# One DMA queue for v, later weight sums, a pause of attention pieces, and warming matmuls in a fused attention and expert kernel

## The chip, the cores and the metric

The kernel runs on one core of a Trainium2 chip. The metric is the device time of one execution in microseconds (us), and quoted times are medians of several executions. "Span" is the time from the first to the last instruction in one profiled execution; it is about 1.8 us shorter than the device time. A ratio is the mean time of one kernel's fast runs over the mean of the other's fast runs of the same rounds, so it isn't quite the ratio of the medians.

## The reference

Polynomial-sketch attention on q, k, v of shape (4, 4, 1088, 32), then four experts on its 4352 rows of 128:

```python
def phi(x):                                   # 8 x 8 = 64 features
    a = np.einsum('rd,bhsd->bhsr', S1, x); b = np.einsum('rd,bhsd->bhsr', S2, x)
    return np.einsum('bhsi,bhsj->bhsij', a, b).reshape(*x.shape[:-1], r * r)
q_p, k_p = phi(q), phi(k)
kv  = np.einsum('bhsf,bhsd->bhfd', k_p, v);  z = np.sum(k_p, axis=2)
x   = (q_p @ kv) / (q_p . z + 1e-6)           # bridged to (4352, 128)
p   = domain_probs / (domain_probs.sum(-1, keepdims=True) + 1e-9)
for e in range(4):
    h = np.maximum(x @ w1[e], 0.0);  out += p[:, e:e+1] * (h @ w2[e])
```

All inputs and the output are float32.

## The kernel before

The experts' work runs in eleven chunks of columns of x (128, 480, 480, five of 512, ...), each in 16 steps. `first(i)` of a step makes h and rectifies it; `second(i - 2)` multiplies by w2. The attention for later columns is a generator of "pieces", and `work()` spends a credit on them between the matmuls of `first`. GpSimd (POOL) forms sums of blocks of w2, which `second` needs from chunk 1 on. PE is TensorE, DVE VectorE, ACT ScalarE and SP SyncE. Names in the traces: kn and kT are k as loaded and transposed, vn is v as loaded, f a projection of k or q and fs its copy, qp the products that make the features of q, kvz the sums over keys, den and num the attention's denominator and numerator, xT the finished columns of x, hid the rectified h, w2s the weight sums, and end the sum of outputs of chunk 0.

The loads at the start. The second half of v goes through ScalarE's queue:

```python
    load_rows(k, 0, "kn")
    load_rows(q, 0, "qn", slice(0, P))
    vn[0] = load_v(0, (nc.sync, nc.scalar))
    ...                                  # domain_probs, ends, rest of q, then w1 and w2 of each expert
    for _ in range(11):
        wp = psum(ps_h, "h")
        nc.tensor.matmul(wp[:, :], warm[:, 0:P], warm[:, :], start=True, stop=True)
```

The key projection, whose output tile comes from PSUM (the memory that these matmuls write), and the end of the first 128 columns of x:

```python
    def keys(b):
        ...
        for gi in range(3):
            key_project(b, gi, psum(ps_f, "f"))   # 32 or 8 matmuls, then a ScalarE copy fs<-f
            yield
    ...
        key_divide(b, kv)
        for _ in attend(b, 0, n, qp):             # den and num matmuls, then DVE: dT, rc, rb, xT
            pass
```

The main loop:

```python
            rate = CHUNKS[m] / NQ * max([0] + [(needed[c] + 4 - done[0]) / (START[c] - gone) for c in range(m + 1, NC)])

            def work():
                credit[0] = min(credit[0] + rate / 2, 2)
                while credit[0] >= 1:
                    credit[0] -= 1
                    piece()

            first(i, work)
            if i > NQ // 2:                       # NQ is 16
                next(to_sum, None)                # one weight sum on GpSimd
```

## Time and profile before

| | before |
|---|---|
| median of the first 3 runs | 502.18 us (500.72 to 502.39) |
| span of the profiled run | 500.6 us |
| TensorE busy | 491.1 us, 98% |
| first matmul on x | 15.11 us |
| stretch at half clock | 15.89 to 19.30 us |
| matmuls wait for DVE's qp products | near 26 us |
| matmuls wait at the entry of chunk 1 | near 39 and 42 us |

TensorE is the bound, so the reader looks for its holes. In the timeline each line has the start, the time taken, the engine, the line of code, the operation, output and input, and in brackets how long the engine had stood and for whom. These lines of the kernel before are from the entry of chunk 1:

```profile
36.58 0.70 DVE L458 STREAM_SHUFFLE qf<-f 128x480 f32<-128x480 f32 x1
...
41.96 0.34 DVE L642 SCALAR_TENSOR_TENSOR end<-o,ends,end 128x128 f32<-128x128 f32 x1
42.22 0.39 DVE L578 SCALAR_TENSOR_TENSOR hid<-h,hid 128x240 f32<-128x240 f32 x1
42.35 0.63 PE L185 MATMUL o<-hid,w_sb 128*64 128x240 f32 x4 [0.58 <-DVE end L642]
```

DVE works on attention pieces (qf and others) from 36.58. The last eviction of chunk 0 (end) comes only at 41.96, behind them, and the matmuls that need its PSUM bank wait.

### The profile page before, as it was taken

To read this page: it belongs to the slowest core of one execution; us is meant where nothing else is said; L and a number is where in the kernel's file an instruction comes from. 1 tells how busy PE (TensorE), PEld (TensorE's weight loads), DVE (VectorE), ACT (ScalarE), POOL (GpSimd) and SP (SyncE) were. 2 spreads that over 40 slices of the span, in tenths; PEclk is the share of its full clock that TensorE was granted. 3 is DMA by queue.
4 is the path that set the end of the run, shared out by engine and by line. 5 is a ranking of instruction groups with operands and counts; after the bars stand their busy time and mean duration, and the time that the engine had idled before them with its cause. 6 is when DMAs were issued, how large, how long until landed. Compare 5 with 4: busy or idle time off the path is not lost.

```text
span 500.6 us, 11017 instructions
## 1 busy us (share of the span) xinstructions
PE 491.1 (98%) x4431; PEld 368.2 (74%) x4431; DVE 324.7 (65%) x751; ACT 243.8 (49%) x487; POOL 228.2 (46%) x259
## 2 busy tenths in 40 slices
PE   8899999999999999999999999999999999999996
PEld 5775888777776657777777777777777777788996
DVE  5659665867667575757667646558656557665642
ACT  3233454545554464544545455445455445566651
POOL 6620334444544263444545344344555355655570
PEclk9899999999999999999999999999999999999999
DMA  7981030021002230021001100021001100110000
GB/s 184 300 289 55 1 91 1 2 85 20 1 2 84 67 89 1 1 85 22 1 2 62 44 1 1 2 85 22 2 1 52 23 1 0 45 22 3 14 3 17
DMA packets 29618, 22.36 MB, mean 45 GB/s; under 512 B 19968, under 2 KB 26752, under 8 KB 29184
## 3 DMA queue, kind: packets, MB, share of 16 engines
q1 hardware_dynamic: 29264, 21.40, 14.9%
q8 instruction: 35, 0.57, 0.5%
q10 hardware_dynamic: 304, 0.26, 0.2%
q14 instruction: 15, 0.12, 0.1%
HBM read 19.35 MB, written 2.31 MB: 43 GB/s over the span
## 4 chain that ended last, share of the span: by engine, by line
PE 94%; DMA 2%; DVE 2%; SPq 0%; issue 0%; ACT 0%; ACTq 0%
PE h L185 47%; PE o L185 39%; PE f L185 4%; PE den L185 2%; DMA w_sb<-in_moe_w_dram 1%; PE num L185 1%; DMA vn<-in_v_dram 1%; DVE qp L409 1%; DVE hid L578 1%; SPq L147 0%; DVE qa L468 0%; DVE qf L458 0%; DVE qb L463 0%; DVE qf L460 0%; DVE end L642 0%
## 5 line engine op out<-in xcount | busy, mean ns | idle before, releaser
L185 PE MATMUL h<-xT,w_sb 128*64 128x512 f32 (+4 forms) x1408 | 299.6, 497 | 1.9 <-DMA w_sb<-in_moe_w_dram 1.6
L578 DVE SCALAR_TENSOR_TENSOR hid<-h,hid 128x256 f32<-128x256 f32 (+6 forms) x432 | 203.6, 472 | 149.3 <-ACT hid L603 141.0
L603 ACT ACTIVATE hid<-h 128x512 f32<-128x512 f32 (+3 forms) x288 | 158.1, 550 | 202.9 <-PE h L185 165.1
L185 PE MATMUL o<-hid,w2s 128*64 128x256 f32 (+3 forms) x1152 | 220.9, 355 | 0.0
L185 PEld LDWEIGHTS h<-xT,w_sb 128*64 128x64 f32 x1408 | 150.2, 138 | 53.0 <-issue 4.7
L185 PE MATMUL o<-hid,w_sb 128*64 128x256 f32 (+3 forms) x864 | 185.0, 356 | 0.6 <-DVE end L642 0.6
L185 PEld LDWEIGHTS o<-hid,w2s 128*64 128x64 f32 x1152 | 131.6, 137 | 31.8 <-issue 0.6
L718 POOL TENSOR_TENSOR ev<-yz,sh 64x256 f32<-64x256 f32 (+3 forms) x72 | 48.4, 673 | 157.8 <-ACT sh L721 155.1
L185 PEld LDWEIGHTS o<-hid,w_sb 128*64 128x64 f32 x864 | 101.4, 137 | 21.1 <-issue 1.6
L706 POOL TENSOR_TENSOR yz<-ev 128x512 f32<-128x512 f32 (+3 forms) x36 | 42.3, 1175 | 86.4 <-ACT ev L709 86.2
L718 POOL TENSOR_TENSOR ct<-ev 128x512 f32<-128x512 f32 (+3 forms) x36 | 42.2, 1173 | 2.8
L718 POOL TENSOR_TENSOR ct<-ct,gate 128x512 f32<-128x512 f32 (+3 forms) x27 | 31.9, 1181 | 2.1
L718 POOL TENSOR_TENSOR total<-total,ct 128x512 f32<-128x512 f32 (+3 forms) x27 | 31.7, 1175 | 2.1
L409 DVE TENSOR_TENSOR qp<-qa,qb 64x352 f32<-64x352 f32 (+2 forms) x44 | 31.3, 712 | 1.0
L185 PE MATMUL o<-w_sb,hid 128*64 128x128 f32 x256 | 24.6, 277 | 0.0
L708 ACT COPY ev<-o 128x512 f32<-128x512 f32 (+3 forms) x36 | 19.3, 537 | 9.7 <-PE o L185 9.2
L185 PEld LDWEIGHTS o<-w_sb,hid 128*64 128x64 f32 x256 | 20.7, 140 | 2.1 <-issue 1.5
L595 ACT ACTIVATE hid<-h 128x256 f32<-128x256 f32 x24 | 9.2, 383 | 24.8 <-PE h L185 24.3
L709 ACT COPY ev<-o 128x512 f32<-128x512 f32 (+3 forms) x36 | 19.4, 538 | 3.0
L348 DVE TENSOR_TENSOR kp<-fs 128x256 f32<-128x256 f32 (+1 forms) x24 | 16.1, 677 | 0.0
L721 ACT COPY sh<-yz 64x256 f32<-64x256 f32 (+3 forms) x36 | 13.7, 379 | 1.6 <-POOL yz L706 0.8
L722 ACT COPY sh<-yz 64x256 f32<-64x256 f32 (+3 forms) x36 | 13.7, 380 | 0.9
(95 smaller groups left out, 246.2 us busy)
## 6 DMA issues: line engine op xcount, KB each, us to landing
w_sb<-in_moe_w_dram SPq DMA_DIRECT2D x8, 512.0 KB, 7.5
gate<-gates SPq DMA_DIRECT2D x3, 1024.0 KB, 4.7
kn<-in_k_dram SPq DMA_DIRECT2D x4, 544.0 KB, 3.9
gate<-gates SPq DMA_DIRECT2D x2, 960.0 KB
vn<-in_v_dram SPq DMA_DIRECT2D x14, 128.0 KB, 5.8
qn<-in_q_dram SPq DMA_DIRECT2D x3, 544.0 KB, 3.6
gate<-gates SPq DMA_DIRECT2D x1, 896.0 KB
out_dram<-ob SPq DMA_DIRECT2D x12, 64.0 KB, 2.0
```

The lines of the kernel that those rows point to most:

```text
L185: nc.tensor.matmul(out(s), weights(s), moving(s), **flags)
L348: eng.tensor_tensor(out=_ap(kps[b], 0, P, 256 * t0 + P * p + 64 * x, [[256, n], [32, 2], [R, 4], [1, R]]), in0=_ap(src, 0, P, off + 4 * x, ...
L409: nc.vector.tensor_tensor(out=qp[p][64 * x : 64 * x + 64, 0:n], in0=qa[64 * p : 64 * p + 64, 0:n], in1=qb[64 * p : 64 * p + 64, 0:n], op=A ...
L578: nc.vector.scalar_tensor_tensor(out=out, in0=src, scalar=0.0, in1=in1, op0=ALU.max, op1=ALU.subtract)
L595: nc.scalar.activation(hd[:, 0 : 2 * n], hp[:, 0 : 2 * n], ACTF.Relu)
L603: nc.scalar.activation(hd[:, n * j : n * j + n], hp[:, 0:n], ACTF.Relu)
L706: add = lambda out, in0, in1, op=ALU.add: nc.gpsimd.tensor_tensor(out=out, in0=in0, in1=in1, op=op)
L708: nc.scalar.copy(_ap(ev, 0, P, 0, [[2 * w, 2], [1, w]]), _ap(a0, 0, P, 0, two))
L709: nc.scalar.copy(_ap(ev, 0, P, w, [[2 * w, 2], [1, w]]), _ap(a1, 0, P, 0, two))
L718: add = lambda out, in0, in1, op=ALU.add: nc.gpsimd.tensor_tensor(out=out, in0=in0, in1=in1, op=op)
L721: nc.scalar.copy(sh[HP:P, 0:w], yz[0:HP, 0, 0:w])
L722: nc.scalar.copy(sh[0:HP, 0:w], yz[HP:P, 1, 0:w])
```

## The change

Its intent is to take four holes out of TensorE's time: let k land alone, keep weight sums away from DVE's products, keep attention pieces away from the entry of chunk 1, and keep the clock up while x is made.

```diff
-    vn[0] = load_v(0, (nc.sync, nc.scalar))
+    vn[0] = load_v(0)                              # all of v on nc.sync
...
+    def keep_warm(n):
+        for _ in range(n):
+            wp = psum(ps_h, "h")
+            nc.tensor.matmul(wp[:, :], warm[:, 0:P], warm[:, :], start=True, stop=True)
+    keep_warm(11)
...
-        for _ in attend(b, 0, n, qp):
+        first = attend(b, 0, n, qp)
+        next(first)                                # den and num
+        keep_warm(4)
+        for _ in first:
             pass
...
-                credit[0] = min(credit[0] + rate / 2, 2)
+                if not NQ <= i < NQ + 2:
+                    credit[0] = min(credit[0] + rate / 2, 2)
...
-            if i > NQ // 2:
+            if i > NQ - 4:
                 next(to_sum, None)
```

More of the change, by code (lines that the diff above doesn't have):

```diff
@@ L93, in load_rows, with load_v @@
         nc.sync.dma_start(d[b][:, part], bass.AP(src.tensor, src.offset + b * H * S * D + c, [[G * D, P], [1, n]]))
-    def load_v(b, engines):
+    def load_v(b):
         t = lpool.tile([P, H * NT * D], F32, tag="vn", name="vn")
@@ L98, in load_v @@
         for a in range(4):
-            engines[a // 2].dma_start(
+            nc.sync.dma_start(
                 _ap(t, 32 * a, 32, 0, [[8 * D, H], [1, 8 * D]]),
@@ L113, in load_batch @@
         load_rows(k, b, "kn")
-        vn[b] = load_v(b, (nc.sync, nc.sync))
+        vn[b] = load_v(b)
         load_rows(q, b, "qn")
@@ L170 @@
         nc.gpsimd.memset(own2[32 * h : 32 * h + 32, h % 2 : h % 2 + 1], 1.0)
-    for _ in range(11):
-        wp = psum(ps_h, "h")
-        nc.tensor.matmul(wp[:, :], warm[:, 0:P], warm[:, :], start=True, stop=True)
+    def keep_warm(n):
[3 more added lines that the diff above has]
+    keep_warm(11)
     turn = [0]
```

## The prediction

> **What bounds the kernel now.** I read the page first, then the chain of waits, then the table of stretches, then the timeline of the stretches that lose time.
>
> ```profile
> PE 491.1 (98%) x4431; PEld 368.2 (74%) x4431; DVE 324.7 (65%) x751; ACT 243.8 (49%) x487; POOL 228.2 (46%) x259
> ...
> PE h L185 47%; PE o L185 39%; PE f L185 4%; PE den L185 2%; DMA w_sb<-in_moe_w_dram 1%; PE num L185 1%; DMA vn<-in_v_dram 1%; DVE qp L409 1%; DVE hid L578 1%; SPq L147 0%; DVE qa L468 0%; DVE qf L458 0%; DVE qb L463 0%; DVE qf L460 0%; DVE end L642 0%
> ```
>
> TensorE is the bound: 98% busy and 94% of the chain. Only its idle time and its slow time can be won. A busy PE is not a PE at its peak, so I also added up the columns of all 4431 matmul records at 1/2.4 us per thousand (the steady stretch from 100 to 150 us needs 49.6 us at this rate and takes 50.1). The sum is 478 us, of which the time from the first matmul to the last takes 496. The lost 18 us lie thus: 5.9 before 15 us, 1.7 between 15 and 19.3, 1.3 between 25 and 29, 1.8 between 35 and 42.5, and the rest is spread at 0.4 to 1.5 per 50 us. The change touches exactly the first four.
>
> The start, from the chain in order of time (start us, us, what):
>
> ```profile
> 1.37 4.75 DMA vn<-in_v_dram
> 6.12 0.02 issue
> 6.13 0.35 SPq L140
> 6.49 0.04 issue
> 6.53 0.70 SPq L147
> 7.23 0.04 issue
> 7.27 0.55 SPq L147
> 7.82 0.04 issue
> 7.86 0.48 SPq L93
> 8.34 0.04 issue
> 8.39 6.58 DMA w_sb<-in_moe_w_dram
> 14.97 0.14 issue
> 15.11 2.12 PE h L185 x24
> ```
>
> Two paths meet at 15.1. The load of the first w1 is issued only at 8.39, because SyncE's queue stood until 6.12 for a transfer of v issued by ScalarE, and lands at 14.97. The other path (k, its projection, key sum, division) gives x at 14.77 (the xT product starts at 14.48 and lasts 0.29). The load wins by 0.2 to 0.3 us only: both must come sooner.
>
> The table of stretches, with the granted clock as the column after POOL, and the two culprits on DVE and POOL in the timeline:
>
> ```profile
> 15.90:19.30 3.40, 3.40 (x26) 2.41 (x24) 0.80 (x4) 1.05 (x3) 2.87 (x5) 0.50 1.11 336
> 25.00:29.00 4.00, 3.82 (x35) 1.92 (x31) 3.17 (x5) 0.77 (x2) 2.84 (x3) 1.00 0.60 234
> 38.40:42.40 4.00, 3.13 (x24) 1.25 (x20) 3.93 (x12) 1.71 (x3) 0.00 (x0) 1.00 0.02 6
> ```
>
> ```profile
> 25.17 2.09 DVE L409 TENSOR_TENSOR qp<-qa,qb 64x480 f32<-64x480 f32 x2
> ```
>
> ```profile
> 25.60 1.13 POOL L491 TENSOR_TENSOR w2s<-w_sb,w2s 128x256 f32<-128x256 f32 x1
> ```
>
> PE is busy all through 15.9 to 19.3, but at half clock: 3.4 us of time, 1.7 of work. From 25 to 29 DVE's products for the second piece of x are late. From 38.4 to 42.4, the first steps of chunk 1, DVE is 98% busy (3.93 of 4.00) and PE is idle for 0.87.
>
> [...] one stretch at 0.50, 3.41 us long in the clock's record, and the window of that length before it (12.48 to 15.89) holds only 0.66 us of den and num and 0.78 of h, 42% busy. [...] a qp product takes 0.64 to 0.66 us at 41 to 47 us with POOL idle, and 1.87 and 2.09 per pair at 22.5 and 25.2 beside weight sums, which themselves go from 0.73 to 1.05-1.14. [...] this k lands near 5.7 (4.5 us after issue), the median of the four k loads is 3.9.
>
> **The change part by part.**
>
> *First v behind k in one queue.* No bytes change: k 544 KB, v 544 KB. Two ScalarE issues (0.81 us) become two SyncE issues (2 x 0.43, from its rows), which fall before the wait that ended at 6.12. [...] with the median 3.9 it lands near 5.0, 0.7 sooner. By the built order of waits, the domain_probs load, which waited for ScalarE's v, now waits for k. SyncE so resumes near 5.0 to 5.3 instead of 6.1, but the later issues wait for the first q and v pieces, and the w1 load for the third v piece, which comes later than before. I put the w1 issue at 7.5 (7.0 to 8.4), its landing at 14.1. On the x path, projection can start at 5.95 (the 11 warm matmuls end at 5.92) against 6.62; the value copies need all of v, which waited until 8.46 before and will not be sooner. Key sums, 72 matmuls in 2.30 us, can start their first half on the first copy. x at 14.1. Gain 0.6, between 0 and 1.1.
>
> *Warming while x is made.* Four bf16 matmuls of 128x512. Eleven took 4.73 us at half clock, 0.43 each; at full clock half of that, 4 x 0.215 = 0.86 us, put into the hole of 1.64 us after num (13.47 to 15.11). They end near 14.3, ahead of x, so on the path they cost nothing. The busy share of that window goes from 42% to (0.66 + 0.78 + 0.86)/3.41 = 67%, or more as h starts sooner. The window from 5.65 to 9.07 was some 80% busy and kept its clock. [...] I take 80% that the half-clock stretch goes. Gain 1.7 x 0.8 = 1.35.
>
> *Weight sums from step fourteen.* The built order shows that this is no real delay: nothing stands on POOL between the gate quotients and the first sum, so the first nine run as before, from about 16 us. What moves is the tail. Before, 13 of the 16 sums stood ahead of the first gather of chunk 1 and ran to 27.84; now 9 do, and the other seven run between gathers after 50 us. The four sums of 24.92 to 27.84 thus leave the second qp pair: 2.09 goes to 1.3, 0.8 less on DVE's way to den. The first pair stays disturbed. PE also arrives sooner, by what it has won, so of the 1.3 lost from 25 to 29 I credit 0.5. The sums for expert 2 are issued by step 24 and used by step 26: some 6 us to spare.
>
> *No attention pieces in steps 16 and 17.* In these steps PE has 2.05 us of work each (eight h of 480 columns and eight small o), while DVE has 1.9 us of rectifying (0.41 + 0.69 + 0.41 and its gaps) and 0.7 per attention piece. Before, qf, qf, qb, qa (2.7 us) stood among them, and the last eviction of chunk 0 behind them, for which PE waited 0.58 by its matmul row. In the built order the eviction now stands right behind step 17, ahead of them. Of the 1.8 us lost from 35 to 42.5 I credit 1.2. The pieces run later; in full steps (3.2 us of PE) there is room, and the rate is worked out anew at every step.
>
> Sum: 0.6 + 1.35 + 0.5 + 1.2 = 3.65. 502.18 - 3.65 = 498.5.
>
> **Rivals.** *The load stays the bound*: v behind k lands later, w1 still waits for it, and PE starts at 15.1 as before. For it: the load's margin, and 1,152 KB to move either way. Then 0.6 is lost: 499.1. *The clock falls all the same*, or falls in another window[...]: then 1.35 is lost: about 499.9. For it: the repeats of before scatter by 1.7 us (500.72 to 502.39), which is just what one such window costs, so before may have escaped it in one run and the gain is partly luck. *DVE becomes the bound at the entry of chunk 1*: pieces put off by two steps bunch up, and den, or the x of chunk 2, is awaited by PE. Against it: 10 or more steps of slack. It would give back 0.5 to 1.
>
> **Range and chances.** All parts good: 1.1 + 1.7 + 1.0 + 1.5 = 5.3, 496.9. One good part failing and the clock staying low: near 500.9. I predict 498.5, 496.9 to 500.9. Two per cent is 10 us, more than all the lost time the change can reach; nothing doubles a wait of that size. Faster 0.01, same 0.98, slower 0.01.
>
> **What would show it.** Right: the w1 landing and x both before 14.7; no 0.5 in the clock's record between 10 and 25 us; k landing near 5; the second qp pair near 1.3 us; PE idle of at most 0.3 from the first h of chunk 1 on for 8 us; POOL idle from about 24 us to the first gather. Wrong: a PE wait on w_sb until 15 or later, a half-clock stretch, a new PE wait on xT or qp past 30 us, or w2s awaited by a matmul.

## The result, and the profile after

The changed kernel takes 498.69 us (498.51 to 499.01, 6 runs) beside 500.94 (500.72 to 502.39, 6 runs) for the kernel before. The ratio is 0.9948, with a 95% interval of 0.9934 to 0.9962: faster by half a per cent, clear of noise, and within 2%. The profiled spans are 496.7 and 500.6 us, a larger difference, because the profiled run of before had the half-clock stretch and most of its runs don't have it (see the experiments).

The page of the changed kernel, and its start from the timeline:

```profile
PE 489.3 (99%) x4435; PEld 367.8 (74%) x4435; DVE 324.8 (65%) x751; ACT 244.0 (49%) x487; POOL 228.2 (46%) x259
```

```profile
4.93 0.43 SPq L140 DMA_DIRECT2D dp<-in_moe_domain_probs_dram  x1
...
7.26 0.43 SPq L124 DMA_DIRECT2D w_sb<-in_moe_w_dram  x1
...
7.55 0.63 ACT L321 COPY vx<-vn 128x512 f32<-128x512 f32 x1 [0.20 <-DMA vn<-in_v_dram]
...
12.58 1.04 PE L176 MATMUL h<-warm 128*128 128x512 bf16 x4
...
14.05 1.53 PE L188 MATMUL h<-xT,w_sb 128*64 128x128 f32 x24 [0.44 <-DVE xT L446]
```

SyncE resumes at 4.93 instead of 6.13, the first w1 load is issued at 7.26 instead of 8.39, and even v is there sooner: its first copy starts at 7.55 instead of 8.46. The first matmul on x moves from 15.11 to 14.05, and it now waits for x, not for the load. The 24 matmuls take 1.53 us instead of 2.12, at full clock.

The stretches that correspond to those of before (columns as there: PE, PEld, DVE, ACT and POOL busy, granted clock, DMA share, GB/s):

```profile
15.90:19.30 3.40, 3.40 (x62) 3.17 (x60) 2.78 (x8) 1.07 (x4) 3.32 (x6) 1.00 1.11 342
21.30:26.00 4.70, 4.28 (x50) 3.12 (x47) 3.82 (x7) 1.15 (x3) 1.93 (x3) 1.00 0.42 110
35.00:39.00 4.00, 4.00 (x35) 2.79 (x33) 3.39 (x9) 2.14 (x4) 0.00 (x0) 1.00 0.31 103
```

The clock is whole, and PE has no hole at the entry of chunk 1. The middle stretch still has one. It's DVE's two pairs of qp products again:

```profile
19.75 2.19 DVE L412 TENSOR_TENSOR qp<-qa,qb 64x480 f32<-64x480 f32 x2
...
22.76 1.67 DVE L412 TENSOR_TENSOR qp<-qa,qb 64x480 f32<-64x480 f32 x2
```

The second pair got quicker (2.09 before), though it still ran beside the ninth sum (22.50 to 23.23), and the first got slower (1.87 before). The profile of before isn't a fair measure here: after its half-clock stretch these products come later (from 22.49 and 25.17 us), when more of the sums are done. The run b_warm, below, shows the old sums at full clock. And at 61 us there is a wait that the kernel before doesn't have at this place:

```profile
61.21 0.37 ACT L344 COPY fs<-f 128x256 f32<-128x256 f32 x1 [0.36 <-PE f L188]
61.63 1.01 PEld L188 LDWEIGHTS f<-sk,kT 128*64 128x64 f32 x32 [0.60 <-ACT fs L344]
```

Two groups of key-projection matmuls follow one another, and the second waits until ScalarE has copied the first out of the only f buffer.

I compared the two traces by the lag of TensorE, which is the time of each matmul's start less the columns done so far at 1000 per 0.417 us (at full clock, the warming matmuls of 512 columns start 0.213 us apart in the changed kernel; they aren't counted themselves). From before to after, the start gives 1.06 us, the clock 1.66, the den wait 0.1, and the entry of chunk 1 1.65; the wait at 61 us takes 0.65 back. The sum is 3.8, which is the difference of the spans (500.58 and 496.74). The clock's term and that of den aren't independent, as b_warm will show.

### The profile page after: what moved, and what is told of

The parts are those of the page before. It is cut to its first block, busy times and chain, and to the rows that moved or that the text cites. A ratio compares the mean times of both kernels' runs of the same rounds, so it can differ in the third digit from the quotient of the medians.

```text
span 496.7 us, 11022 instructions
## 1 busy us (share of the span) xinstructions
PE 489.3 (99%) x4435; PEld 367.8 (74%) x4435; DVE 324.8 (65%) x751; ACT 244.0 (49%) x487; POOL 228.2 (46%) x259
## 4 chain that ended last, share of the span: by engine, by line
PE 98%; DVE 1%; issue 0%; ACT 0%; DVEq 0%
PE h L188 49%; PE o L188 40%; PE f L188 5%; PE den L188 2%; PE num L188 1%; PE h L176 1%; DVE qp L412 1%; ACT fs L344 0%; DVE qa L471 0%; DVE end L648 0%; DVE end L644 0%; DVE xT L446 0%; DVE kvz L374 0%; DVE warm L135 0%; DVE s_hl L212 0%
## 5 line engine op out<-in xcount | busy, mean ns | idle before, releaser
L188 PEld LDWEIGHTS h<-xT,w_sb 128*64 128x64 f32 x1408 | 148.2, 137 | 52.2 <-issue 12.9
L188 PEld LDWEIGHTS o<-hid,w2s 128*64 128x64 f32 x1152 | 133.1, 137 | 29.0 <-issue 2.7
L412 DVE TENSOR_TENSOR qp<-qa,qb 64x352 f32<-64x352 f32 (+2 forms) x44 | 30.2, 687 | 1.1
```

The costliest lines, as they stand in the source:

```text
L188: nc.tensor.matmul(out(s), weights(s), moving(s), **flags)
L412: nc.vector.tensor_tensor(out=qp[p][64 * x : 64 * x + 64, 0:n], in0=qa[64 * p : 64 * p + 64, 0:n], in1=qb[64 * p : 64 * p + 64, 0:n], op=A ...
```

## The experiments

Twelve kernels ran, in three sets of four, each set with the kernel before in the same rounds; all gave correct results. The names start with "b" where one part was added to the kernel before, and with "a" where the changed kernel was edited. My theory after the result: the four parts each act on their own hole, warming only insures against a chance event, the sums miss most of their aim, and the pause costs a new wait. The rivals stand in the expectations.

All these runs count, but the list of clocks splits them. Of the 29 runs of before in the three sets, 20 had a mean granted clock of 0.998 or more and took 500.50 to 501.04 us. The other 9 had 0.996 or 0.997 and took 501.85 to 502.61, with one at 504.01. I call the first "undisturbed"; their means in the three sets are 500.69, 500.79 and 500.82. The changed kernel itself ran in none of these sets, which ran at three other times on three chips; its 498.72 (mean of its six runs) is from the first comparison. There the four quicker runs of before average 500.86, so the level moved by at most 0.17 us, and differences against 498.72 are good to about that.

**b_warm: only the four warming matmuls.**

```diff
-        for _ in attend(b, 0, n, qp):
+        first = attend(b, 0, n, qp)
+        next(first)
+        keep_warm(4)
+        for _ in first:                            # keep_warm as in the change
```

> The kernel before plus the four warming matmuls alone. My theory (they only prevent a half-clock window that falls by chance): no repeat shows a clock below 0.999 and all lie near 500.8 us, so the gain is about 1.6 us in those repeats of before that have the window (2 of its 6 so far, at 502.2 to 502.4) and nothing in the others; mean gain 0 to 0.8 us. Rival (TensorE is faster after warming whatever the window): every repeat gains over 1 us against before's quickest, below 499.8. Second rival [...]: clocks of 0.997 and times of 502.3 still occur.

Measured: 500.76 us (500.50 to 500.98), ratio 0.9984 (0.9964 to 1.0004), and all six clocks at 0.998 or more. Its runs equal the undisturbed ones of before (500.69), so warming by itself gave no speed. What went is the half-clock stretch: over all seven warmed kernels without a large wait later on (36 runs with the changed kernel's six), no run has a clock below 0.998, against 9 of 29 of before.

Its profile also shows the old order of sums at full clock. There both pairs of products are slow:

```profile
20.73 2.25 DVE L413 TENSOR_TENSOR qp<-qa,qb 64x480 f32<-64x480 f32 x2
23.78 2.09 DVE L413 TENSOR_TENSOR qp<-qa,qb 64x480 f32<-64x480 f32 x2
```

To compare the den wait in all traces I take the growth of TensorE's lag from the 100th to the 200th matmul after the first on x. It is 1.73 us here and 1.36 in before. So the half-clock stretch costs 1.66 us where it occurs, but without it TensorE waits 0.37 longer for den. The 1.3 that is left fits the two groups of before in this set, which lie 1.34 apart (502.03 without the run of 504.01, and 500.69).

**a_nowarm: the changed kernel without them.**

```diff
-        keep_warm(4)
```

> The changed kernel without the four warming matmuls. Theory: some repeats (about 4 in 10, as of before) show a clock of 0.997 or less and lie 1.2 to 1.7 us above the others; those with 0.998 or more lie at 498.7, like the changed kernel's. Rival (v's earlier start alone keeps the window busy enough): all repeats at 498.7. Rival (warming gains in every repeat): all near 499.8 or more.

Measured: 499.17 us (498.64 to 499.82), one run of five at 0.997 (499.82). The four others average 499.00, near the changed kernel's 498.72. So the drop still occurs without warming, as the theory said, and in what ran warming excluded it. That the earlier start makes it rarer isn't shown: one in 5 is too few against 9 in 29. The means differ by 499.16 - 498.72 = 0.44 us, but the one disturbed run makes only 0.16 of that. The other 0.28 lies between undisturbed runs of two occasions and isn't explained; b_warm showed no such gain.

The traces also show how full TensorE was before the clock fell. The stretches of full and half clock that both begin and end in a record last 10.24, 3.413 and 481.279 us in before and 491.519 in the changed kernel: 3, 1, 141 and 144 times 3.4133 us. So I laid windows of this length from the changes of clock; that windows also lie where the clock didn't change is my estimate. The table has the window that held the making of x. "Busy" is the share of time in which matmul records lie, whose ends are modelled. "Filled" counts the columns at 1000 per 0.417 us instead, those of each matmul spread evenly over its record.

| kernel | window ends at (us) | busy | filled | clock after it |
|---|---|---|---|---|
| b_pause | 15.43 | 39% | 25% | half |
| before | 15.89 | 42% | 31% | half |
| b_v | 14.64 | 47% | 32% | half |
| b_sums | 15.09 | 47% | 32% | half |
| a_nowarm | 14.19 | 52% | 41% | full |
| b_warm | 15.67 | 66% | 52% | full |
| a_vback, a_hold, a_nopause | 14.5 to 14.9 | 74% | 56 to 60% | full |
| changed kernel | 15.71 | 87% | 76% | full |

In this table the windows followed by half clock were filled to 25 to 32%, and those that kept full clock to 41% (a_nowarm) or more. Busy time doesn't order the windows: 47% lost the clock (b_v and b_sums), and elsewhere three of 45% kept it (in a_one and a_hold_one, ending at 259.76 and 258.20, and at the end of a_num). That the filled share decides, and at which share, isn't shown. That the chance lies in where the windows fall is an estimate: I slid a window of this length over the start in two traces. In a_nowarm it is filled to less than 35% (between the table's 32 and 41) in a quarter of its positions (one run of five was disturbed), and in b_warm it never falls below 42%.

**b_v: only v on one queue.**

```diff
-    vn[0] = load_v(0, (nc.sync, nc.scalar))
+    vn[0] = load_v(0, (nc.sync, nc.sync))
```

> The kernel before with v's second half moved to the other queue alone. Theory: the first matmul on x starts near 14.05 us instead of 15.11, as in the changed kernel, so 1.0 us off before's undisturbed 500.8: 499.8. Rival (the waits downstream on the second piece of x absorb it, since DVE's products set that point): 0 to 0.3 us.

Measured: 500.42 us (499.93 to 501.28), ratio 0.9978 (0.9957 to 0.9999). The first matmul on x starts at 13.98, as expected, but the five undisturbed runs average 500.29, only 0.40 below before.

**a_vback: v back on two queues in the changed kernel.**

```diff
-            nc.sync.dma_start(
+            (nc.scalar if a > 1 and b == 0 else nc.sync).dma_start(     # a: quarter of v
```

> The changed kernel with v's second half back on ScalarE's queue. Theory: the first matmul on x starts at 15.0 us again instead of 14.0 to 14.4, and nothing after it takes that up: 499.5 to 499.8 with every clock at 0.998 or more. Rival (part is taken up by later waits, as v's move alone brought only 0.4 us over undisturbed repeats): 498.9 to 499.2, the den wait at 24 us being shorter than 0.6 us by what the start is later.

Measured: 499.67 us (499.21 to 499.95), 0.87 more on the mean (499.59 against 498.72). The first matmul on x is back at 14.87. Here the start is worth what it is by itself, and nothing later takes it up. Over all profiles this first matmul starts at 14.85 to 15.15 with two queues (five traces) and at 13.98 to 14.37 with one (eight; a ninth, a_one, had 14.81 and got its full clock only at 7.18). The first transposition of k started at 5.40 to 5.81 us in the five traces with v's second half on the other queue, and at 4.92 to 5.30 in the nine with all of v behind k. Why b_v won only 0.40 isn't settled. Its undisturbed runs scatter by 0.7 us, and none of them was profiled. Its one trace, of a disturbed run, speaks against the rival: its den wait (1.40) is as long as before's (1.36), and its span is 1.1 us shorter than that of before, 499.5 against 500.6, so nothing later took the start up.

**b_sums: only the later weight sums.**

```diff
-            if i > NQ // 2:
+            if i > NQ - 4:
```

> The kernel before with only the later weight sums. Theory from the two traces: the first nine sums do not move, the second pair of qp products gets 0.4 us quicker, gain 0 to 0.4 us in repeats without the half-clock window (500.4 to 500.9). Rival (as predicted): 0.8 us off the pair and 0.5 off the time. A loss above 0.3 us would speak for a wait on the sums.

Measured: 500.46 us (500.14 to 501.41), ratio 0.9980 (0.9959 to 1.0001); the five undisturbed runs average 500.38, 0.31 less than before. Its pairs of products:

```profile
22.24 1.94 DVE L409 TENSOR_TENSOR qp<-qa,qb 64x480 f32<-64x480 f32 x2
...
24.98 1.34 DVE L409 TENSOR_TENSOR qp<-qa,qb 64x480 f32<-64x480 f32 x2
```

The second pair is free of the sums, and the first isn't. That is the theory's picture. Its den wait (lag growth as under b_warm) is 0.66 us instead of before's 1.36, both with the half-clock stretch. At full clock the six traces with the later sums and without the hold have 1.26 to 1.31, against 1.73 in b_warm. So the sums take about 0.45 off that wait at full clock. On the time, the 0.31 isn't clear of noise: the interval of the ratio includes 1.

**a_hold: GpSimd waits for the second piece of x before the sums of expert 1.**

```diff
+            if i == NQ + 1:
+                held = cpool.tile([P, 1], F32, name="held")
+                nc.gpsimd.tensor_copy(held[:, :], xT[:, START[2] - 1 : START[2]])
             if i > NQ - 4:
                 next(to_sum, None)
```

> The changed kernel with GpSimd made to wait for the second piece of x (a one-column copy of it) before the weight sums of expert 1, so that no sum runs beside the qp products. Theory [...]: the pairs of 2.19 and 1.67 us go to about 1.3 each, den starts 1.1 to 1.3 us sooner than 23.79 or without a wait, and 0.5 to 1.0 us is won: 497.7 to 498.2. Rival (qp is slow for another reason, PE or the DMA traffic): the pairs stay above 1.8 and the time at 498.7.

Measured: 497.80 us (497.67 to 498.32), ratio 0.9939 (0.9926 to 0.9953), 0.8 us less than the changed kernel on the mean (497.90).

```profile
19.96 1.31 DVE L412 TENSOR_TENSOR qp<-qa,qb 64x480 f32<-64x480 f32 x2
...
22.07 1.34 DVE L412 TENSOR_TENSOR qp<-qa,qb 64x480 f32<-64x480 f32 x2
```

Both pairs now take the time of undisturbed products (0.64 to 0.66 us each in before at 41 to 47 us, with GpSimd idle), and TensorE's wait for qp is gone from its list of waits (den wait 0.14 by lag). DMA traffic is as in the changed kernel (327 and 313 GB/s from 19.7 to 22.0 us), so the rival falls: the sums slowed the products. In the changed kernel the first two qp products took 2.19 us and the two sums behind them 1.14 and 1.15 each (here the pair takes 1.31 and a sum 0.73), and the four lie between 19.75 and 22.54, the 2.8 us of one after the other. In before, b_warm and the changed kernel each slowed product ended 0.51 to 0.52 us after the sum ahead of it, and each slowed sum 0.58 to 0.59 after the product ahead of it (20 of 20).

This also shows why the change's own move is weak. GpSimd ran ahead of the program's steps: in the changed kernel, which issues the sums four steps later, the first started at 15.92 us (16.74 before) and the ninth at 22.50 (22.79). With something to wait for, in a_hold, the fifth started at 27.38 instead of 18.80.

**b_pause: only the pause of two steps.** The edit is the two lines of the diff on the credit.

> The kernel before with only the pause of two steps. Theory: 1.65 us of waits between 35 and 42.5 us go, and 0.65 comes back as a wait of the second key projection for the ScalarE copy of the first, since two pieces now fall behind one another: net gain 1.0 us, 499.8. Rival (as predicted, no give-back): 1.2 to 1.7 us, 499.1 to 499.6, and no wait on fs above 0.5 us at 55 to 70 us.

Measured: 500.90 us (499.75 to 501.44), ratio 0.9980 (0.9956 to 1.0003). Four of its six runs were disturbed, so the median hides the effect. The two undisturbed ones average 499.90 against before's 500.69, 0.79 less. The four disturbed ones average 501.09, against 502.03 for the four disturbed runs of before in this set without the one at 504.01: 0.94 less. From the list of TensorE's waits (us in total, times, longest):

```profile
PE f L185 <- ACT fs L341: 0.9, 2, 0.5
```

Before has one such wait, of 0.5 us; with the pause there are two. The net gain is near the 1.0 that the theory expects, though two undisturbed runs are few.

**a_nopause: the changed kernel without the pause.**

```diff
-                if not NQ <= i < NQ + 2:
+                if True:
```

> The changed kernel without the pause in steps 16 and 17. Theory: the waits at the entry of chunk 1 (for ScalarE's rectified columns and for the last eviction of chunk 0, 1.0 to 1.7 us) come back and the wait at the second key projection of 0.63 us near 61 us goes: 499.5 to 499.9. Rival (as predicted, with no give-back): 499.9 to 500.4.

Measured: 499.58 us (499.48 to 500.05), 0.98 above the changed kernel on the mean (499.70 against 498.72), every clock at 0.998 or more. Its waits:

```profile
PE o L188 <- DVE end L648: 0.6, 1, 0.6
...
PE f L188 <- ACT fs L344: 0.5, 1, 0.5
...
PE h L188 <- ACT hid L609: 0.3, 1, 0.3
```

The eviction and the rectified columns are waited for again, and one of the two waits on fs is gone. That agrees with the lag of before and after, by which the pause gains 1.65 and costs 0.65.

**a_one: at most one piece between two groups of matmuls.** This tries to part the two key projections.

```diff
-                while credit[0] >= 1:
+                if credit[0] >= 1:
```

> The changed kernel with at most one attention piece between two groups of matmuls, so the second key projection no longer follows the first at once. Theory (the wait of 0.6 us at 61.6 us comes of two pieces in a row that share one PSUM buffer): the waits of f for fs shrink by 0.4 to 1.2 us in the first 200 us; 497.6 to 498.3. Rival (some other wait takes its place, pieces being late for chunk 2 or 4): 498.7 or more, with waits on xT.

Measured: 515.79 us (514.19 to 516.21), ratio 1.029: a miss. The rival came true, with pieces late for their chunks:

```profile
PE den L188 <- DVE qp L412: 8.1, 5, 3.2
PE h L188 <- DVE xT L446: 2.5, 2, 1.2
```

TensorE waits near 140 and 262 us until the attention of a whole piece of x is done, and each time the clock fell to half for 6.83 us (two windows); the mean granted clock of the run is 0.985, against 1.000 for the changed kernel.

**a_hold_one: a_hold and a_one together.** 

> Both of the last two edits on the changed kernel. If they are independent the gains add: 496.9 to 497.7. If both are the same slack, no better than the better of the two.

Measured: 513.86 us, for the same reason as a_one.

**a_num: the second key projection in another PSUM bank.**

```diff
-            key_project(b, gi, psum(ps_f, "f"))
+            key_project(b, gi, psum(ps_n, "num") if gi == 1 else psum(ps_f, "f"))
```

> The changed kernel with the second of the three key projections put into the num bank of PSUM instead of the f bank. Theory: two projections in a row no longer share a bank, both waits of 0.63 us (near 61 and 168 us) go, 1.0 to 1.3 us won: 497.4 to 497.7. Rival (ScalarE or DVE is the bound there): the waits move to the next product and 498.3 or more is left.

Measured: 497.42 us (497.21 to 497.59), ratio 0.9922 (0.9904 to 0.9940), 1.32 less than the changed kernel on the mean. No wait for fs is left in TensorE's list, neither near 61 us nor near 168 us, where the kernel before had one too. So the new wait was the shared bank, and neither ScalarE nor DVE.

**a_hold_num: the held sums and the second bank.**

> The held weight sums and the num bank together, on the changed kernel. If the gains of 0.9 and 1.0 to 1.3 us are independent: 496.5 to 496.9, 0.8 per cent below before. If they share slack: near 497.5.

Measured: 496.25 us (495.95 to 496.53), ratio 0.9898 (0.9880 to 0.9916). On the mean it's 2.5 less than the changed kernel, where the parts gave 0.8 and 1.3: they add, and a little more. This version beats both kernels. After the first matmul on x at 14.16 us, its lag has no single jump above 0.17 us.

## Why the prediction was right or wrong

The time, 498.69, lies in the range and near 498.5, and "within 2%" was right. This isn't proof of each step. The steps, in the prediction's order:

- **First v behind k, 0.6 us: right in kind, the size open.** Profile 1.06, taken back alone 0.87, added alone 0.40. The term that failed is the value copies that "will not be sooner": they came 0.9 sooner (7.55 against 8.46), so the x path moved whole. The w1 load, which I feared as the rival bound, was not waited for.
- **Warming, 1.35 us: right in kind, the term mis-sized.** The stretch was avoided (b_warm's window was 66% busy, predicted 67%). But I multiplied by the chance that warming works (0.8, my estimate) and forgot the chance that the kernel before has the stretch at all: two of the first three runs had times of disturbed ones, so I took 502.18 for the base, and in the later sets 9 of 29 were disturbed. I also took the whole 1.7, of which 0.37 comes back in the den wait. By 9/29 of 1.34 us the gain over before is about 0.4 us on the mean, an estimate. The remark under the second rival, that the scatter of 1.7 us is one such window, was the right reading, and it should have changed the sum.
- **Weight sums, 0.5 us: near right at the wait, less shown on the time.** The step that the sums don't move but only their tail does was right (the ninth sum starts at 22.50, then POOL is idle for 25.56 us). The profiles of before and after differ by only 0.1 at the den matmuls, because the one has the half-clock stretch and the other doesn't; at full clock the sums took about 0.45 off the wait. On the time, 0.31 alone. The sign of 1.3 us for the second pair was missed (1.67). At full clock the pairs come sooner and meet more of the undelayed sums: the first pair takes 2.25 in b_warm and 2.20 in a_vback, where v is on two queues, so v's earlier start isn't the reason.
- **The pause, 1.2 us: net 0.8 to 1.0.** The waits that went sum to 1.65, so I was too careful there, but "in full steps there is room" missed that two pieces can follow one another and share one PSUM buffer. The rival for bunching named den or the x of chunk 2, neither of which was waited for; the cost was 0.65 at the key projection.
- **Sum.** The means of the first six runs differ by 501.33 - 498.72 = 2.6. The parts give the same if v and the pause are taken back (0.87 + 0.44 + 0.31 + 0.98 = 2.6), but 1.9 if they are added alone (0.40 and 0.79), so this agreement proves little. My 3.65 was the gain over a disturbed run (profiled spans: 3.8). By medians the base was 1.2 us too high (502.18 against 500.94) and the gain 1.4 too large (3.65 against 2.25). That the time came so close to 498.5 is luck: two errors cancelled.

## What to carry to other kernels

Before adding up gains, ask whether the time they start from is one state or a mixture: a list of clocks per run showed two groups about 1.3 us apart that a median of three had mixed. Here an engine that ran ahead wasn't delayed by issuing its work later in the program (the ninth sum started at 22.50 us, 22.79 before); the wait in a_hold did delay it (the fifth from 18.80 to 27.38). When two profiles are compared part by part, check that they are in the same state: a half-clock stretch at one place changed how long TensorE waited at the next (den wait 1.36 us in before, 1.73 in b_warm). Where pieces of work are paced by a credit, pausing them makes them come in pairs afterwards, so look at which buffer two neighbours share.
